# Accumulating DMAs for part of the output sums, idle products up to the first r product, and a new order of operations

## The chip, the cores and the metric

The program runs on one core of a Trainium2 chip. The metric is device microseconds (us) of one execution; the kernel before was timed three times. In the profile TensorE is PE (its weight loads PEld), VectorE is DVE, ScalarE is ACT, GpSimd is POOL and SyncE is SP. SP issues nearly all DMAs; POOL issues the accumulating ones.

## The reference, cut to what matters

Three layers follow one another on 4 sequences of 576 tokens with 512 channels, all in float32.

```python
# 1. attention with 8 heads of 64 channels, each token sees itself and the 63 tokens before it
attn = softmax(mask(q @ k.T / 8));  x = attn @ v                       # (4, 576, 512)
# 2. token shift, then a gated feed-forward
x_prev = shift(x);  xk = mu_k*x + (1-mu_k)*x_prev;  xr = mu_r*x + (1-mu_r)*x_prev
k = relu(xk @ w_k)                                                     # (4, 576, 1024)
x2 = sigmoid(xr @ w_r) * ((k*k) @ w_v)                                 # (4, 576, 512)
# 3. gate from a causal convolution of 5 taps, then two products
gate = sigmoid(sum_j conv_w[j] * x2 shifted by 4-j)
out = (gate * (x2 @ w_val)) @ w_out
```

## The kernel before, in words

Everything is kept transposed: channels on the 128 partitions, tokens along the row. The 2304 tokens are cut into five blocks, t = 0 of 256 tokens and t = 1 to 4 of 512. A unit of attention is one block and one pair of heads, 20 units u0 to u19 (u0 to u3 belong to block 0). A unit goes through these steps, each with a name in the plan: `qk` (scores, PE), `top` (row maximum, DVE), `exp` (ACT), `eps` and `rec` (reciprocal of the row sums), `norm` (DVE), `tp` (transposes on PE into the PSUM tile `at`), `pt` (copy out of PSUM), `pv` (product with v), `x` (copy of the result into `xT`). In block 0 the second half of `at` takes the result of `pv`. From `xT` the steps `a` and `xm` mix each token with the one before. `r`, `h` and `v` are the three products of layer 2. In block 0 they are plain float32 products; in the other blocks each operand is split in two parts (hi, lo) and three products are added.

Weights come in raw and are put together by `w_r ld` (load), `g` (ACT), `t` and `s` (DVE); `w_r s` of the first piece and `xm` of the first two channel groups are what the first `r` product needs.

Layer 3 works on one sequence b = 0 to 3 at a time, as `val{b}` (x2 times w_val) and `out{b}` (times w_out). In `val0` to `val3` and `out0` to `out2` the product is done as seven products of quarter size, m1 to m7, of 12 matmuls each, in `seven` (line 859). They add up in two PSUM banks "u" and "v". What must be used twice is copied from bank u to SBUF: three copies per sequence, `outu` 0, 1 and 2 into the tile `ou` (`valu` for val). For out, three of the four output quarters (00, 11, 01) are then bank v plus one of those copies, added on DVE (`o`, line 951); the quarter 10 is bank u alone, copied by ACT (line 953). `os` stores a quarter of 288 KB. The next sequence's `outu` i waits until the `o` that read the old copy is done. `out3` is a plain product of 96 matmuls and ends the kernel.

The gate of sequences 0 to 2 is worked out early; that of sequence 3 is made late, partly by four accumulating DMAs (`acc`, line 848, 576 KB each) that POOL issues.

No scheduler runs: the table `SLOT` holds a place in the program for each step, the steps are emitted in that order, and each engine executes its own in that order. `Plan.run` walks over the steps with estimated durations, but only for one purpose: where PE would wait longer than `WAIT` ns, `fill` emits idle products (128x128, operands zero, result never read) that keep PE busy, one for every `PASS` ns of the gap less 250 ns. Before, the idle products write to the tile `scores` and end when the first unit of block 1 takes that tile.

Of the kernel before, what the change touches and what calls it, by code (L numbers as in the profile page):

```python
# [36 lines left out]
BY_DMA = (3, 4)  # L37
BIG = 3.0e38
# [4 lines left out]
    'first': '32',  # L43
# [6 lines left out]
    'ldc': '15',  # L50
    'mu': '17',
    'omu': '56',
    'pg': '51',
    'wc0': '69 75 96',
    'wc': '98',
    'first_x': '1',
    'ldqk': '7 3 9 12 13 21 44 81 111 166 195 232 265 295 335 368 393 421 445 495',
    'ldv': '18 10 24 27 46 117 164 185 269 271 298 331 365 389 422 441 499 492 522 577',
    'qk': '20 16 31 34 38 72 106 134 182 227 257 291 330 363 388 417 440 477 491 521',
    'top': '26 22 33 39 48 82 112 149 228 293 296 333 349 376 403 448 450 489 504 535',  # L60
    'exp': '29 25 36 42 59 89 122 168 249 297 311 340 362 384 416 452 457 505 511 545',
    'eps': 'v35 p30 p43 p50 p70 p102 p132 p179 p259 v305 v318 p345 v373 v396 v426 p458 p466 p512 v523 p553',
    'rec': '37 40 55 57 80 103 171 190 262 307 319 355 379 407 432 460 473 517 538 555',
    'norm': '41 45 58 66 92 123 180 196 270 309 320 357 382 410 435 462 485 518 548 583',
    'tp': '47 60 68 85 101 130 189 231 275 314 334 366 392 419 444 480 496 525 558 586',
    'pt': 'a49 v62 a73 a86 a108 a116 a144 a152 a203 a199 a235 a247 a281 a279 a322 a321 a350 a338 v381 a378 a404 '
        'v408 a425 a428 v465 a464 v484 a483 v509 v510 a537 a529 a563 v562 a602 a600',
    'pts': '53 64 78 90 120 155 207 252 287 325 353 383 411 429 469 486 513 541 565 604',
    'pv': '54 65 79 91 125 178 222 255 289 326 358 386 414 437 475 488 519 543 568 632',
    'x': 'v61 a71 v87 v97 a160 a206 a246 a264 a292 v346 a372 a400 v418 v455 v478 a493 a536 v551 a629 v719',  # L70
    'mask': '211 238 278 323 339 370 397 424 447 487 501 531',
    'edge': '218 261 283 329 348 374 401 427',
    'a': 'a83 a100 a110 a118 a230 a237 a272 a276 a352 a356 a436 v439 v494 a498 v610 a614 a693 v764 v768 a797',
    'xm': '88 107 119 126 254 242 300 284 390 367 451 443 520 524 624 620 734 785 776 823',
    'xlo': '93 113 124 129 266 274 327 290 434 415 479 463 609 606 673 634 765 788 783 832',
    'carry': '137 214 260 361 398 459 528 628',
    'r': '94 121 95 115 109 127 139 147 369 395 405 423 590 581 593 599 686 744 751 760 863 871 883 889',
    'sig': '136 138 150 154 399 406 433 438 594 596 603 626 697 752 761 767 873 879 890 909',
    'h': '153 162 165 173 143 148 158 170 176 198 194 205 201 213 210 217 294 301 308 316 337 342 351 377 500 '
        '507 482 532 552 547 561 569 643 672 699 720 695 708 726 737 816 829 802 835 845 859 852 878',  # L80
    'relu': 'v169 a181 a159 a184 a202 a212 a219 a223 a303 a310 v315 v344 v343 a371 v387 a402 v508 v515 v506 a544 '
        'a559 a566 a580 v584 v663 v683 a709 a727 v713 a729 v743 v746 a827 a838 v810 a847 a854 a864 v866 v885',
    'sbuf': '186 188 216 225',
    'slo': 'a193 v191 a221 a229 341 364 385 420 550 567 597 601 707 739 749 759 851 862 877 891',
    'v': '239 251 234 244 263 286 273 277 430 449 446 461 514 527 454 467 635 654 611 625 660 679 607 616 766 '
        '786 780 789 809 824 772 796 919 930 896 905 924 933 901 912',
    'x2': '282 253 299 304 470 471 546 476 661 652 688 627 794 801 830 803 934 914 938 921',
    'st': '336 268 394 391 472 474 549 574 664 655 689 656 805 804 839 843 936 916 947 943',
    'xhi': 'a258 a267 v312 v288 v431 a412 v468 v453 a608 a588 v631 a623 a755 a787 v779 a826',
    'cut': '241 280 360 442 503 619',  # L90
    'shi': '328 347 375 409 534 560 575 585 687 732 738 748 840 848 870 886',
    'sq': 'a332 a359 a380 v413 a540 a564 a595 v592 v696 a736 a740 a754 v846 a857 v874 v888',
    'staging': '0',
    'w_r ld': '19 23',
    'w_r g': '52 74',
    'w_r t': '63 76',
    'w_r s': '67 99',
    'w_r hi': 'v131 a156',
    'w_r lo': '141 161',
    'w_k ld': '84 28 77 114',  # L100
    'w_k g': '140 104 146 177',
    'w_k t': '133 105 128 174',
    'w_k s': '145 135 157 183',
    'w_k hi': 'a197 v167 a240 a215',
    'w_k lo': '208 175 245 220',
    'w_v ld': '151 142 163 192',
    'w_v g': '209 187 243 224',
    'w_v t': '204 172 236 226',
    'w_v s': '233 200 248 256',
    'w_v hi': 'a317 v302 a324 a285',  # L110
    'w_v lo': '354 313 456 306',
    'wide_x': '250',
    'turn': '880',
    'turn_s': '940',
    'turn_w': '834 894',
    'w_val ld': '497 589 578 651',
    'w_val room': '571 636 618 674',
    'w_val g': '572 637 640 675',
    'w_val t': '554 579 582 612 605 622 642 644 648 646 591 667 669 682 670 665 680 710 711 712',
    'w_val s': '576 641 645 678',  # L120
    'w_val hi': 'a613 a650 a684 a714',
    'w_val lo': '615 671 698 721',
    'w_val st': '621 617 668 677 685 702 733 735',
    'w_out ld': '647 681 706 731',
    'w_out room': '701 723 757 775',
    'w_out g': '703 724 793 791',
    'w_out t': '700 716 717 715 718 705 741 742 763 762 773 821 822 831 825 756 815 818 817 849',
    'w_out s': '704 728 820 812',
    'w_out hi': 'v747 a769 v833 v853',
    'w_out lo': '753 771 837 869',  # L130
    'w_out st': '750 758 777 774 836 842 875 872',
    'wv2': '898 899',
    'wo2': '900 897 917 945',
    'ldx': '884 941 957 1011',
    'gbuf': '881 942 1020 1082',
    'ldg': '882 958 1060',
    'xhi_': 'a931 a906 a907 a904 v918 a928 a959 a991 a966 a964 a997 a988 a993 a1076 a1032 a1038 a1088 a1073 a1100 '
        'a1162 a1119 a1118 a1171 a1161',
    'xlo_': '935 908 910 915 954 939 963 1008 968 974 1005 998 1023 1084 1052 1061 1095 1081 1106 1181 1144 1137 '
        '1178 1163',  # L140
    'xsum': '902 903 911 926 960 961 975 984 1017 1030 1065 1071 1111 1115 1154 1158',
    'val': '937 944 948 951 955 965 969 973 983 989 999 1006 1021 1028 1041 1053 1063 1080 1087 1096 1102 1110 '
        '1121 1141 1148 1166 1187 1182',
    'valu': 'a946 v952 a962 a978 a1002 a1013 a1048 a1079 a1092 a1127 a1157 a1176',
    'valc': '949 967 970 979 994 1019 1027 1035 1072 1097 1104 1113 1132 1180 1208 1191',
    'gv': '950 971 972 992 1003 1025 1031 1045 1090 1109 1107 1129 1183 1201 1209 1194',
    'ghi_': 'v953 a1009 a980 a982 a985 a1007 a1004 a1039 a1066 a1029 a1036 a1042 a1056 a1068 a1122 a1136 a1124 '
        'a1147 a1145 a1174 v1175',
    'glo_': '956 1018 1015 986 990 1010 1014 1049 1069 1067 1040 1057 1075 1078 1135 1150 1185 1159 1156 1188 '
        '1177',  # L150
    'gsum': '976 981 996 1000 1033 1037 1054 1062 1120 1142 1165 1170',
    'out': '977 1046 995 1012 1016 1024 1034 1059 1074 1070 1091 1108 1116 1128 1138 1155 1160 1173 1179 1192 '
        '1197 1202 1211 1207 1213 1216 1220 1219 1221',
    'outu': 'a987 a1001 a1022 a1064 a1077 a1112 a1149 a1169 a1184',
    'o': '1055 1026 1044 1043 1086 1123 1130 1146 1168 1186 1198 1203 1214 1217 1222 1224',
    'os': '1058 1051 1047 1050 1134 1153 1133 1151 1172 1190 1200 1205 1215 1218 1223 1225',
    'tap': '1083 1089 1099 1085 1093 1101 1098 1125 1140 1103 1117 1139',
    'part': '1094 1114 1131 1152',
    'acc': '1105 1126 1143 1167',
    'gate': '1164 1189',  # L160
    'ghi': 'a1193 a1196 a1210 v1204',
    'glo': '1195 1199 1212 1206',
    'cld': '481 587 676 781 813 868',
    'ctap': '502 526 530 533 557 490 516 539 542 556 598 630 633 639 658 638 649 653 657 659 690 692 722 730 770 '
        '691 694 725 745 778 795 798 806 807 811 790 792 799 800 808 828 841 844 850 856 855 858 860 861 865 '
        '887 893 895 913 925 892 920 922 923 927',
    'cgate': '570 662 782 814 867 929',
# [1046 lines left out]
```

## Time and profile before

| | |
|---|---|
| three runs | 422.95, 423.63, 421.28 us; median 422.95 |
| the profiled execution | 423.3 us, of which its span (first to last instruction) is 421.5 us |
| instructions | 9145 |
| PE busy | 410.9 us (97% of the span) |
| DVE busy | 351.9 us (83%) |
| ACT busy | 256.7 us (61%) |
| POOL busy | 22.5 us (5%) |
| mean granted TensorE clock | 0.996 |
| DMA | 77.69 MB, mean 184 GB/s |

Busy is the time in which an engine executes something; a busy PE can still be slow, when its granted clock is 0.5 (1.2 GHz in place of 2.4 GHz) or when its matmuls are small. The chain that ended last gives PE 83% and DVE 13% of the span.

### The profile page before, as it was taken

Reading aid. Unit: us, or ns where it says so; the run is one execution under the profiler, and the core shown is the slowest. Engines: PE = TensorE matmul, PEld = TensorE weight load, DVE = VectorE, ACT = ScalarE, POOL = GpSimd, SP = SyncE. Lnnn points to the kernel's source line nnn. Section 1 sums busy time; section 2 is a strip of 40 time slices with the busy share of each in tenths; the row PEclk is TensorE's granted clock in tenths of the full one; section 3 lists DMA queues with packets and bytes.
Section 4 is the critical chain, followed back from the end, with each engine's and each line's share of the span. In section 5 each row is a group of like instructions: output and inputs, shape, how many; then the busy total and the mean of one; then the engine's idle time right before and its main releaser. Section 6 shows DMA issues by size and latency. Waiting matters only on the chain.

```text
span 421.5 us, 9145 instructions
## 1 busy us (share of the span) xinstructions
PE 410.9 (97%) x3746; PEld 354.8 (84%) x3746; DVE 351.9 (83%) x511; ACT 256.7 (61%) x585; POOL 22.5 (5%) x62
## 2 busy tenths in 40 slices
PE   8789999999999999999999999999999999999996
PEld 6578888888888888888888888888888899999996
DVE  3899998988989799458978996988584999999970
ACT  4899997789996175765334645154223284577721
POOL 2114101000002000000000000000000000001000
PEclk9899999999999999999999999999999999999999
DMA  8998925333432522072375434434997913616622
GB/s 306 407 366 320 381 64 166 104 117 104 131 113 98 208 103 77 2 286 89 116 261 210 137 157 155 161 152 153 343 427 286 400 69 114 225 35 155 176 86 112
DMA packets 24714, 77.69 MB, mean 184 GB/s; under 512 B 2528, under 2 KB 3296, under 8 KB 22624
## 3 DMA queue, kind: packets, MB, share of 16 engines
q1 hardware_dynamic: 23952, 74.74, 48.5%
q0 software_dynamic: 576, 2.36, 2.9%
q8 instruction: 29, 0.48, 0.4%
q14 instruction: 13, 0.11, 0.1%
q10 hardware_dynamic: 144, 0.00, 0.0%
HBM read 53.90 MB, written 20.84 MB: 177 GB/s over the span
## 4 chain that ended last, share of the span: by engine, by line
PE 83%; DVE 13%; issue 1%; ACT 1%; ACTq 0%; POOL 0%; DVEq 0%; POOLq 0%
PE h L603 21%; PE v L603 21%; PE r L603 10%; PE at L497 4%; PE ao L512 4%; PE scores L433 4%; PE v L627 3%; PE h L627 3%; PE out L979 3%; PE out2m L873 3%; DVE x L771 2%; DVE gq L771 2%; PE val3m L873 2%; PE r L627 2%; DVE early L914 1%; DVE xt L761 1%
## 5 line engine op out<-in xcount | busy, mean ns | idle before, releaser
L603 PE MATMUL h<-x,wk 128*128 128x512 f32 x384 | 90.7, 391 | 0.0
L603 PEld LDWEIGHTS h<-x,wk 128*128 128x128 f32 x384 | 71.5, 188 | 14.8
L603 PE MATMUL v<-sh,wv 128*128 128x512 f32 x256 | 81.1, 390 | 0.0
L603 PEld LDWEIGHTS v<-sh,wv 128*128 128x128 f32 x256 | 48.1, 188 | 10.0
L603 PE MATMUL v<-sl,wv 128*128 128x512 f32 x128 | 49.8, 389 | 0.0
L603 PE MATMUL r<-x,wr 128*128 128x512 f32 x192 | 45.4, 391 | 0.0
L603 PEld LDWEIGHTS r<-x,wr 128*128 128x128 f32 x192 | 35.7, 188 | 7.3
L804 DVE SCALAR_TENSOR_TENSOR early<-early,wc 128x576 f32<-128x576 f32 x48 | 38.2, 810 | 3.1 <-ACT early L802 2.7
L476 ACT ACTIVATE s<-s,m 128x128 f32<-128x128 f32 x96 | 37.2, 397 | 4.6 <-DVE m L465 4.6
L603 PEld LDWEIGHTS v<-sl,wv 128*128 128x128 f32 x128 | 24.0, 188 | 4.9
L504 ACT ACTIVATE pt<-at 128x512 f32<-128x512 f32 x28 | 16.4, 601 | 13.6 <-PE at L497 13.6
L654 ACT ACTIVATE rk<-h 128x512 f32<-128x512 f32 (+1 forms) x23 | 12.1, 538 | 17.9 <-PE h L603 15.8
L563 DVE SCALAR_TENSOR_TENSOR xm<-xT,omu,xm 128x512 f32<-128x512 f32 x32 | 22.5, 744 | 0.6 <-POOL xT L569 0.6
L684 DVE TENSOR_TENSOR sl<-rk,sh 128x1024 fp32r<-128x1024 f32 x16 | 19.4, 1219 | 3.9 <-ACT rk L682 3.8
L706 DVE TENSOR_TENSOR sgs<-v,sgs 128x512 f32<-128x512 f32 (+1 forms) x20 | 12.5, 632 | 10.9 <-PE v L603 10.9
L678 ACT ACTIVATE sh<-rk 128x1024 fp32r<-128x1024 f32 x16 | 16.9, 1055 | 6.8 <-DVE rk L656 6.7
L512 PEld LDWEIGHTS ao<-pt,vt 128*64 128x64 f32 x512 | 16.2, 138 | 5.5 <-issue 2.8
L586 DVE TENSOR_TENSOR x<-xm,x 128x1024 fp32r<-128x1024 f32 x16 | 19.4, 1219 | 1.2 <-ACT x L583 1.1
L486 DVE TENSOR_TENSOR s<-s,m 128x1024 f32<-128x1024 f32 x16 | 19.5, 1219 | 0.2
L768 ACT ACTIVATE x<-xt 128x576 fp32r<-128x576 f32 x15 | 10.0, 677 | 15.4 <-DVE xt L761 9.4
L476 ACT ACTIVATION_READ_ACCUMULATOR s<-s,m 128x1 f32 x96 | 18.8, 196 | 0.0
L512 PE MATMUL ao<-pt,vt 128*64 128x64 f32 x512 | 18.4, 225 | 0.0
(200 smaller groups left out, 857.5 us busy)
## 6 DMA issues: line engine op xcount, KB each, us to landing
qk<-qk SPq DMA_DIRECT2D x16, 544.0 KB, 5.2
vt<-vh SPq DMA_DIRECT2D x16, 512.0 KB, 4.9
xb<-x2d SPq DMA_DIRECT2D x4, 1152.0 KB, 7.2
out_t<-st SPq DMA_DIRECT2D x15, 288.0 KB, 2.8
x2d<-sgs SPq DMA_DIRECT2D x16, 256.0 KB, 3.5
w_out<-w SPq DMA_DIRECT2D x8, 512.0 KB, 3.5
w_val<-w SPq DMA_DIRECT2D x8, 448.0 KB, 4.5
wk<-w_val SPq DMA_DIRECT2D x2, 1792.0 KB, 11.8
```

Of the source, the lines that this page charges most:

```text
L433: PE.matmul(a["ps"][rows, h, o:o + W + HW], lhsT=a["q"][heads[h], c * HW:(c + 1) * HW], rhs=a["k"][heads[h], c * HW:c * HW + W + HW], star ...
L476: ACT.activation(out=s, in_=scores()[:, c // n2, c % n2, :] if by_pe else s, func=AF.Exp, scale=D ** -0.5 if by_pe else 1.0, bias=l(0)[:, ...
L486: lambda: V.tensor_tensor(out=a["s"], in0=a["s"], in1=l(1).unsqueeze(2).to_broadcast(sq), op=ALU.mult))
L512: PE.matmul(a["o"][heads[h], c * W:(c + 1) * W], lhsT=a["v"][:, c, heads[h]], rhs=a["pt"][:, h, c * W:(c + 1) * W], start=True, stop=True)
L563: V.scalar_tensor_tensor(out=m, in0=xT[:, f, :n], scalar=omu[:, c:c + 1], in1=m, op0=ALU.mult, op1=ALU.add)
L586: lambda E: E.tensor_tensor(out=dst(1), in0=src(), in1=f32(dst(0)), op=ALU.subtract))
L603: PE.matmul(ps, lhsT=a, rhs=b[:, kt, :], start=(kt == 0 and i == 0), stop=(kt == nk - 1 and i == 2))
L627: PE.matmul(Ps[key][:, :n], lhsT=ws(kt), rhs=x()[:, kt, :], start=kt == 0, stop=kt == nk - 1)
L678: ACT.activation(out=Ss[t][0][:, f, :n], in_=rk(), func=AF.Square)
L684: lambda E: E.tensor_tensor(out=Ss[t][1][:, f, :n], in0=rk(), in1=f32(Ss[t][0][:, f, :n]), op=ALU.subtract))
L804: V.scalar_tensor_tensor(out=o, in0=x, scalar=c, in1=o, op0=ALU.mult, op1=ALU.add)
L873: PE.matmul(z[bank][:, j, :HS], lhsT=lhs, rhs=rhs, start=new and kt == 0 and e == 0, stop=kt == 1 and e == 2, skip_group_check=not new)
```

## The change: what it does

It does four things.

1. For sequences 1 and 2 (`ADDED`) the quarters 00, 11 and 01 are no longer added on DVE. ACT copies bank v to SBUF, SP stores it as before, and a new step `oa` on POOL then issues a DMA that adds the SBUF copy `ou` onto the stored result in DRAM. `oa` waits for the landing of that store, and the next sequence's `outu` waits for `oa`.
2. Idle products go to an unused part of the second half of `at`, and are emitted until the first `r` product or the first `pt` of block 1 is reached.
3. `WAIT` goes from 700 to 400 and `PASS` from 430 to 250: shorter gaps are filled, and a gap of the same length gets more products. `WARM` stays at 900.
4. Nearly every place in `SLOT` is new, and some steps that DVE or ACT can both do have moved from one to the other.

```diff
+ADDED = (1, 2)
...
-    WAIT, PASS, WARM = 700, 430, 900
+    WAIT, PASS, WARM = 400, 250, 900
...
-            if "at" not in Q:
-                Q["at"] = pa.tile([P, 2, TB], F32, tag="at", name="at")
...
-        prev = lambda h, p: [({"val": "gv", "out": "o"}[mul], b - 1, h, p)] if b else []
+        prev = lambda h, p: [({"val": "gv", "out": "oa" if b - 1 in ADDED else "o"}[mul], b - 1, h, p)] if b else []
...
-                if u:
+                if u and b not in ADDED:
                     V.tensor_tensor(out=o, in0=ps(), in1=u(), op=ALU.add)
                 else:
                     ACT.activation(out=o, in_=ps(), func=AF.Copy)
...
             store(b, h, p, [slice(0, 2)])
+            if u and b in ADDED:
+                op(("oa", b, h, p), "pool", 1000, [("os", b, h, p), *deps], lambda: G.dma_start(
+                    out=out[2 * b + h, :, 2 * p:2 * p + 2, :], in_=u(), accum_op=ALU.add), moves=1750)
...
     def first_idle():
-        idle["ps"] = Q["scores"] = pq.tile([P, 2, TB], F32, tag="qk", name="scores")
+        Q["scores"] = pq.tile([P, 2, TB], F32, tag="qk", name="scores")
+        Q["at"] = pa.tile([P, 2, TB], F32, tag="at", name="at")
...
-        if any(k in Ps for k in [("r", 0, m) for m in range(NF)]) or HP in A and "ps" in A[HP] or n <= 0:
+        if any(k in Ps for k in [("r", 0, m) for m in range(NF)]) or any("pt" in A[u] for u in A if u >= HP) or n <= 0:
             return
         for _ in range(n):
-            PE.matmul(idle["ps"][:, 0, :P], lhsT=warm, rhs=warm, start=True, stop=True)
+            PE.matmul(Q["at"][:, 1, TA:TA + P], lhsT=warm, rhs=warm, start=True, stop=True)
```

Of `SLOT`, the orders that the prediction speaks of, written out as sequences of steps on an engine up to the first `r` product (u0 to u3 are the units of block 0):

```
PE  before: qk u1, qk u0, qk u2, qk u3, qk u4, tp u0, pv u0, tp u1, pv u1, tp u2, qk u5, pv u2, tp u3, pv u3, r
PE  after:  qk u1, qk u0, qk u2, qk u4, qk u3, tp u0, pv u0, tp u1, pv u1, tp u2, qk u5, pv u2, tp u3, pv u3, r
DVE before: top u1, top u0, top u2, eps/rec u0, top u3, rec u1, norm u0, norm u1, top u4, rec u2, omu, rec u3, norm u2,
            x u0, pt u1, w_r0 t, norm u3, w_r0 s, w_r1 t, rec u4, top u5, x u2, xm 0.0r
DVE after:  omu, top u1, top u0, eps/rec u1, norm u1, top u2, rec u0, norm u0, top u3, top u4, rec u2, x u0, norm u2,
            pt u1, rec u3, w_r0 t, norm u3, x u1, eps u4, pt u2, rec u4, w_r0 s, top u5, xm 0.0r
```

And in layer 3 the quarters, `oa` and the last products:

```
POOL after: acc 0, oa1 00, acc 1, acc 2, oa1 01, oa1 11, acc 3, oa2 00, oa2 01, oa2 11
last products before: out3 00, 01, 10, 11      after: out3 01, 00, 11, 10
val0 on DVE before: x differences S1 and S2 of val1, lo of val1's first pair, quarter 11      after: S1, S2, quarter 11
```

## Rows read from the trace of the kernel before

**Rows 1.** Five stretches of the span: length, each engine's busy us (instructions), clock, DMA
```profile
0.00:23.10 23.10, 17.67 (x395) 13.35 (x395) 14.35 (x36) 16.29 (x66) 3.78 (x16) 0.93 0.94 359
23.10:331.60 308.50, 308.50 (x2729) 257.96 (x2728) 261.40 (x366) 190.10 (x440) 14.96 (x41) 1.00 0.51 184
331.60:404.60 73.00, 71.76 (x532) 70.74 (x531) 72.62 (x106) 46.94 (x74) 3.72 (x5) 1.00 0.48 147
404.60:417.60 13.00, 12.95 (x98) 12.71 (x96) 3.56 (x6) 2.66 (x5) 0.00 (x0) 1.00 0.25 94
417.60:421.50 3.90, 0.00 (x0) 0.00 (x0) 0.00 (x0) 0.69 (x2) 0.00 (x0) 1.00 0.40 147
```

**Rows 2.** Timeline, PE at the start: start, duration, engine, operation, count, [idle before]
```profile
0.99 2.93 PE L1158 MATMUL scores<-sgs 128*128 128x128 f32 x12 [0.99 <-POOL sgs L302]
...
4.26 0.89 PE L433 MATMUL qk<-early 64*32 64x96 f32 x32
...
8.07 0.56 PE L433 MATMUL qk<-early 64*32 64x96 f32 x32
...
11.82 0.53 PE L433 MATMUL scores<-qk 64*32 64x96 f32 x21 [0.71 <-issue]
...
16.07 1.05 PE L512 MATMUL at<-pt,sgs 128*64 128x64 f32 x16 [1.18 <-DVE pt L505]
...
17.05 1.12 PE L497 MATMUL at<-ident,xm 128*128 128x128 f32 x4
...
19.99 0.69 PE L512 MATMUL at<-pt,rk 128*64 128x64 f32 x16
...
20.60 0.66 PE L497 MATMUL at<-ident,xm 128*128 128x128 f32 x4
...
23.08 1.99 PE L627 MATMUL r<-x,words 128*128 128x256 f32 x8
```

**Rows 3.** Timeline, DVE at the start: one row for each kind of step
```profile
5.26 0.69 DVE L467 TENSOR_REDUCE first_m<-qk 128x4 f32<-128x512 f32 x1 [2.11 <-PE qk L433]
...
12.39 1.22 DVE L467 TENSOR_REDUCE m<-scores 128x8 f32<-128x1024 f32 x1
...
13.73 0.17 DVE L484 RECIPROCAL first_m<-first_m 128x4 f32<-128x4 f32 x1
...
13.95 0.67 DVE L486 TENSOR_TENSOR xm<-xm,first_m 128x512 f32<-128x512 f32 x1
...
14.99 0.42 DVE L518 COPY xT<-at 128x256 f32<-128x256 f32 x1 [0.37 <-PE at L497]
...
17.13 1.22 DVE L345 SCALAR_TENSOR_TENSOR words<-words,x 128x1024 int32<-128x1024 int32 x1
...
22.32 0.87 DVE L563 SCALAR_TENSOR_TENSOR x<-xT,omu,x 128x256 f32<-128x256 f32 x2
```

**Rows 4.** Chain of waits, ACT's exponentials of the first two units: start, us, line, count
```profile
6.25 2.91 ACT xm L476 x15
```

**Rows 5.** Timeline, PE late: the two longest waits
```profile
332.67 1.85 PE L873 MATMUL val0m<-x,wk 128*128 128x288 f32 x12 [0.74 <-ACT early L885]
...
385.00 0.40 PE L873 MATMUL out2m<-gq,wr 128*128 128x288 f32 x1 [0.34 <-DVE gq L771]
```

**Rows 6.** Line L848, the accumulating DMAs of the gate: POOL's issue in ns, and landing
```profile
L848 POOL DMA_DIRECT2D gate<-tt x2: 859/938/1016, 376.1 to 387.6; - x2
...
DMA to landing us min/median/max: 4.8/4.8/4.9
```

**Rows 7.** Line L931 from 414 us, then from 418.2 us: the last stores' issue to landing
```profile
DMA to landing us min/median/max: 2.1/2.1/2.1
...
DMA to landing us min/median/max: 1.7/1.8/1.8
```

**Rows 8.** Timeline, ACT at the end: copies of the last quarters out of PSUM
```profile
416.03 0.65 ACT L989 ACTIVATE st<-out 128x576 f32<-128x576 f32 x1 [4.20 <-PE out L979]
...
417.58 0.71 ACT L989 ACTIVATE st<-out 128x288 f32<-128x288 f32 x2 [0.90 <-PE out L979]
```

More of the change, by code (lines that the diff above doesn't have):

```diff
@@ L953, in go @@
                     ACT.activation(out=o, in_=ps(), func=AF.Copy)
-            op(("o", b, h, p), "dve" if u else "act", v_ns(QN) if u else p_ns(QN), [*deps, *room(b, h, p)], go)
+            by_v = u and b not in ADDED
+            op(("o", b, h, p), "dve" if by_v else "act", v_ns(QN) if by_v else p_ns(QN), [*deps, *room(b, h, p)], go)
             store(b, h, p, [slice(0, 2)])
+            if u and b in ADDED:
+                op(("oa", b, h, p), "pool", 1000, [("os", b, h, p), *deps], lambda: G.dma_start(
+                    out=out[2 * b + h, :, 2 * p:2 * p + 2, :], in_=u(), accum_op=ALU.add), moves=1750)
         seven("out", b, "g", gq, lambda c, j: w2["w_out"](c, j)[:, 1:], WO, "turn_s", use)
@@ L1144, in tile_kernel @@
         early_gate(n, SPLIT[n // 2], n % 2)
-    idle = {}
     def first_idle():
-        idle["ps"] = Q["scores"] = pq.tile([P, 2, TB], F32, tag="qk", name="scores")
+        Q["scores"] = pq.tile([P, 2, TB], F32, tag="qk", name="scores")
+        Q["at"] = pa.tile([P, 2, TB], F32, tag="at", name="at")
     op("idle", "none", 0, ["warm"], first_idle)
     def fill(t, n):
-        if any(k in Ps for k in [("r", 0, m) for m in range(NF)]) or HP in A and "ps" in A[HP] or n <= 0:
+        if any(k in Ps for k in [("r", 0, m) for m in range(NF)]) or any("pt" in A[u] for u in A if u >= HP) or n <= 0:
             return
         for _ in range(n):
-            PE.matmul(idle["ps"][:, 0, :P], lhsT=warm, rhs=warm, start=True, stop=True)
+            PE.matmul(Q["at"][:, 1, TA:TA + P], lhsT=warm, rhs=warm, start=True, stop=True)
     plan.fill = fill
```

237 rows, old and new, of the table SLOT are left out of this document.

## The prediction, made before the changed kernel was run

> **What bounds the kernel now.** I read the stretches of the span first. In them the reader is to see four parts: a start of 23.1 us in which PE is busy for 17.67, with a mean clock of 0.93; 308.5 us in which PE has not one idle 0.01 us and the full clock; 73 us in which PE has 71.76 and DVE 72.62, so that both are full; and an end of 13.0 us of products plus 3.9 us after the last of them [rows 1]. The work of PE is the same before and after (idle products aside), so whatever this change does to the time, it does by PE's waits: 5.4 us in the start, 1.24 us in the 73, and the 3.9 behind the last product. In the middle nothing can be gained, only lost.
>
> Then I read the timeline of the start. The first r product begins at 23.08 us, and from there PE never waits [rows 1, 2]. So the start is worth what the first r product moves. Ahead of it PE runs idle products from 0.99 (12 records in 2.93 us: a float32 product shows as two, so six products), then the scores of the units; the scores of one unit take 0.89 us at first and 0.56 later [rows 2]: the first ones run at 1.2 GHz, the later ones at 2.4. Later the clock falls once more: a pv of 16 products takes 1.05 us at 16.07 and 0.69 at 19.99, a tp 1.12 at 17.05 and 0.66 at 20.60 [rows 2]. A mean clock of 0.93 over 23.1 us is about 3.2 us at half speed [rows 1]. Ahead of the fall PE had waited much: 1.18 us just before, and 0.71 us in the middle of the scores of u4, with nothing that released it [rows 2].
>
> **The change part by part.**
>
> *More idle products in the first gap.* The number is the gap less 250 ns, divided by PASS. Six at 430 means that 2.58 to 3.01 us were to be filled; at 250 that makes 10 to 12, I take 11. Five more, 0.49 us each (2.93 / 6) at 1.2 GHz, are 2.4 us; as the last of them and the scores behind them come close to the rise of the clock, the next scores take 0.56 in place of 0.89. I take 1.5 us by which the first unit's row maximum starts later: 6.8 us in place of 5.26 [rows 2, 3]. Bounds: 0.5 (the clock has risen early) and 2.4. This is the one place where the change puts work on the path that sets the start. What waits behind is the first maximum on DVE, and ACT's exponentials behind that.
>
> *New order up to the first r product.* PE's list differs in one place only (scores of u4 ahead of those of u3); DVE's and ACT's lists are new. I walk them with the old durations. Maximum of u1: 6.8 + 0.69 + 0.17 = 7.7. Exponentials: two units took 2.91 [rows 4], so 1.45 each, and that of u1 ends at 9.1. That frees the buffer for the scores of u2 (0.56 and its masks, 0.9): 10.1. From there DVE is the queue that counts: maximum of u2, rec and norm of u0, 0.86 + 0.17 + 0.67, until 11.9; then it waits for the scores of u3, which PE reaches behind those of u4 (about 1.4) at 12.4. Then without a pause: top u3 0.86, top u4 1.39, two rec 0.34, two x 0.84, two norm 1.34, two pt (same width as norm) 1.34, w_r0 t 0.67 (an estimate, as norm), eps and rec of u4 0.34, w_r0 s 1.22, top u5 1.39, xm 0.87 [rows 3]. That is 10.6 us, and r starts at 23.0. Before, the same queue began 1.5 us earlier and lost it in waits: it did norm u0 only behind top u3, and waited for PE at half clock. So the later start and the better order cancel: **0.0 us**. Low bound: what PE lost at half clock on pv and tp alone is 0.36 + 0.46, with the scores between them about 1.2, and the wait of 0.71 [rows 2]; if both go and the first gap costs nothing, -1.9. High bound: the 1.5 is not made good and the wait of 0.71 comes again, now ahead of u3's maximum too: +2.2.
>
> *Idle products in the later gaps.* They fill what PE waits anyway, with 250 ns left free each time, so they cost nothing as long as the gaps come as planned; if a gap is shorter, the cover is gone, and one product too many costs 0.2 us at 2.4 GHz. They hold the clock, which is in the walk above already.
>
> *The order from 23 to 331 us.* Before, no wait in 308.5 us, with DVE at 85% and ACT at 62% [rows 1]. A step moved between them changes nothing as long as it comes in time; whether each does is not to be seen in this trace. I take **0.0**, with bounds of 0 and +1.2 (as much as PE waits in the 73 us where DVE is as full as PE).
>
> *The six sums taken off DVE.* Six additions of some 0.75 us, 4.5 us in all, leave DVE, and six copies of 0.65 [rows 8] go to ACT, which is busy for 46.94 of the 73 us [rows 1] and has room. But PE is busy for 71.76 of the same 73, so at most 1.24 us can come of it. PE's longest wait there (0.74 at 332.67) is for a copy of its own m7 result ahead of m4, in sequence 0, where nothing is moved. That of 0.34 at 385.00 is for DVE [rows 5] and goes. In val0 the quarter 11 now comes ahead of a longer DVE step, which takes a smaller wait. **-0.4 us**, bounds -1.24 and 0.
>
> *The accumulating DMAs.* Six issues on POOL at 0.94 us, on an engine that is busy for 3.72 of 73 us [rows 1, 6]. Each waits for a store (landing 2.1 to 4.8) and must land before the next sequence's copy into the same part of `ou`. The trace has no accumulation onto DRAM; the nearest rows are a store of the same 288 KB (2.1, [rows 7]) and an accumulation of 576 KB into SBUF (4.8, [rows 6]); I take 4.8, the nearer kind. Copy, store, issue and accumulation: 0.65 + 4.8 + 0.94 + 4.8 = 11.2 us. For quarter 00 there are ten products of some 1.6 us in between (1.85 with the tail of the last matmul, [rows 5]), 16 us: hidden. For quarters 01 and 11 of sequence 1, POOL holds them behind two `acc`, and between their issue and the copy that needs the room lie four to five products, about 7 us against 0.94 + 4.8 = 5.7: hidden by little. Those of sequence 2 have 13 us of out3 and 3.9 us behind them and free no buffer. **0.0**, bounds 0 and +3.
>
> *The end.* The last store is now quarter 10 whole; before it was quarter 11 in two halves. Before: 417.58 + 0.71, then a landing of 1.75. After: 0.65, then 2.1 [rows 7, 8]. **+0.2 us**.
>
> Sum: 0.0 + 0.0 - 0.4 + 0.0 + 0.2 = -0.2 us on the 423.3 of the profiled execution, of which 421.5 are the span. That execution is 0.35 above the median of the runs shown; on the median it makes 422.95 - 0.2 = **422.7 us**.
>
> The row says that POOL's issues took 0.86 to 1.02 us and landed in 4.8 to 4.9, beside a DVE that is busy for 72.62 of 73 us [rows 1, 6]. The Trainium skill ("SBUF — State Buffer", section "A bandwidth-pool intuition that's wrong (but worth ruling out)") speaks against such DMAs: GpSimd can't write their descriptors while certain VectorE copies hold the shared port, and one of 620 ns took 3100. By that rule each could land some 2.5 us later (an estimate from that page), and the margin for quarters 01 and 11 would be gone; by the row it is not so here. It is why the third rival has any chance beyond a few per cent.
>
> **The rivals.**
>
> *Faster start.* The idle products keep PE at 2.4 GHz from 6 us on, the first unit starts hardly later, and the 0.71 goes. For it: pv and tp at half clock lie in line ahead of the first r product. Against it: five more products at 1.2 GHz stand ahead of the first scores. -1.9 - 1.24 + 0.2 = -2.9: 420.0 us.
>
> *Slower start.* One mechanism: the products added to the first gap. They hold PE until about 6 us although the first scores could start at 3.9, and every step of DVE behind moves with them, as its queue has no pause left to take it up. It decides against the change from the point where the delay of the first maximum is above 1.5 us and the wait in u4's scores comes too. +2.2 + 0.2 = +2.4: 425.3 us.
>
> *Accumulations late.* The copies `outu` 1 and 2 of sequence 2 find `ou` not yet free, and PE stops between m6 and m4 of out2. For it: the margin of 1 to 2 us. Against it: landings in rows 6 hardly vary. +3.0 - 0.2: 425.7 us.
>
> *Doesn't do what it says.* The idle products share a PSUM bank with the results of pv; if they wait for the reads of it, the clock still falls. Then the start costs about 1.2 more: 423.9 us, still no change by the measure below.
>
> **How the numbers follow.** Forecast 0.46 and the last rival 0.06, both within 0.5% (2.1 us, about what a measurement of this kernel can tell from no change: 420.8 to 425.1); faster start 0.29; slower start 0.12; accumulations late 0.07. So faster 0.29, same 0.52, slower 0.19. The forecast's own range is -1.5 to +1.5, 421.2 to 424.2. For 8 in 10 it must take in most of the faster case and the edge of the slower ones: 419.8 to 425.0.
>
> **What would show it.** First scores at about 5.7 us in place of 3.9, first row maximum at 6.8; over 40 records of idle products in place of 22, and no stretch at half clock between 6 and 23 us; the first r product at 22 to 24 us; PE without a wait from there to 331 us; PE's waits from 331 to 405 us near 0.8 in place of 1.24; six new DMAs on POOL that land in 4.8 us or less, and no copy into `ou` that waits for one; some 0.2 us more behind the last product. The forecast is wrong if r starts before 21.5 or after 24.5, or if PE waits for over 1 us anywhere between 24 and 405 us.

## The result, and the profile after

After the change the kernel takes 427.75 us (median of 4 runs, 426.06 to 429.29), beside 422.99 (4 runs) for the kernel before on the same chip: 1.0127 of it, 95% interval 1.0085 to 1.0168. Forecast were 422.7 us and a range of 419.8 to 425.0: the change costs 4.8 us, where no difference was the likeliest case.

The profiled execution took 429.22 us, its span 427.4. Its stretches, cut at the same work as those of before [rows 1]; the columns are the stretch, its length, busy us (instructions) of PE, PEld, DVE, ACT and POOL, the granted clock, the DMA share and GB/s:

```profile
0.00:28.90 28.90, 23.41 (x428) 18.80 (x428) 15.57 (x38) 16.08 (x67) 2.63 (x15) 0.82 0.88 326
28.90:338.75 309.85, 309.85 (x2731) 257.97 (x2728) 259.69 (x367) 191.48 (x441) 7.79 (x40) 1.00 0.51 178
338.75:410.40 71.65, 70.86 (x532) 70.62 (x531) 69.20 (x100) 51.20 (x80) 7.22 (x9) 1.00 0.62 175
410.40:423.40 13.00, 12.94 (x98) 12.70 (x96) 2.48 (x5) 2.67 (x5) 1.76 (x2) 1.00 0.58 146
423.40:427.40 4.00, 0.00 (x0) 0.00 (x0) 0.00 (x0) 0.65 (x1) 0.00 (x0) 0.99 0.31 117
```

Against [rows 1] the start is 5.8 us longer, at a clock of 0.82 in place of 0.93; the 308.5 us are 1.35 longer although PE is busy in every one of them; the 73 us are 1.35 shorter; the end hardly moves. So one stretch holds the loss, and two small ones cancel.

The timeline of PE in the start (start, duration, operation, count, [idle before]):

```profile
0.99 4.18 PE L1161 MATMUL at<-sgs 128*128 128x128 f32 x22 [0.99 <-POOL sgs L304]
5.11 0.31 PE L425 MATMUL qk<-low,one 64*64 64x256 bf16 x4
...
6.61 2.05 PE L1161 MATMUL at<-sgs 128*128 128x128 f32 x16
...
12.34 0.19 PE L429 MATMUL qk<-low,one 64*64 64x64 bf16 x1 [1.42 <-issue]
...
14.43 1.22 PE L1161 MATMUL at<-sgs 128*128 128x128 f32 x4 [0.69 <-ACT pt L504]
15.58 1.12 PE L512 MATMUL at<-pt,sgs 128*64 128x64 f32 x16
...
19.20 2.08 PE L1161 MATMUL at<-sgs 128*128 128x128 f32 x8 [0.78 <-DVE pt L505]
21.21 1.12 PE L512 MATMUL at<-pt,sgs 128*64 128x64 f32 x16
...
27.43 0.94 PE L1161 MATMUL at<-sgs 128*128 128x128 f32 x6 [1.01 <-ACT xT L519]
28.30 0.69 PE L512 MATMUL at<-pt,rk 128*64 128x64 f32 x16
28.91 0.92 PE L627 MATMUL r<-x,words 128*128 128x256 f32 x3
```

Line L1161 holds the idle products. The reader is to look at the last three groups of them: each has a wait in front of it, for a copy out of the tile `at`, and only then runs, ahead of the `pv` for which the gap was. The gap stays and the products come on top: 15.58 - 14.43 = 1.15, then 2.01, then 0.87, together 4.0 us. The clock is at 1.2 GHz all the same from the first of them on (`pv` takes 1.12; [rows 2] have 1.05 at that clock and 0.69 at 2.4).

DVE, which the prediction took for the queue that counts from the maximum of u3 on, stands still behind PE there (the first row is that maximum, the others are its three longest pauses up to the first r product):

```profile
13.27 0.69 DVE L469 TENSOR_REDUCE first_m<-qk 128x4 f32<-128x512 f32 x1 [1.99 <-PE qk L435]
...
16.82 0.42 DVE L518 COPY xT<-at 128x256 f32<-128x256 f32 x1 [1.25 <-PE at L512]
...
18.46 0.69 DVE L505 COPY pt<-at 128x512 f32<-128x512 f32 x1 [0.61 <-PE at L497]
...
23.42 0.42 DVE L518 COPY xT<-at 128x256 f32<-128x256 f32 x1 [3.01 <-PE at L497]
```

Late, PE keeps one wait of the two longest of [rows 5], the one of sequence 0; that for DVE is gone. The second fence holds the new DMAs (their issue in ns min/median/max, first and last start, and their landing), the third the landing of the last three stores, the fourth ACT at the end.

```profile
339.87 3.46 PE L873 MATMUL val0m<-x,wk 128*128 128x288 f32 x24 [0.79 <-ACT early L885]
```

```profile
L958 POOL DMA_DIRECT2D out_t<-ou x6: 858/875/1204, 382.2 to 415.7; - x6
DMA to landing us min/median/max: 4.4/6.0/7.2
```

```profile
DMA to landing us min/median/max: 1.8/1.8/2.1
```

```profile
423.42 0.65 ACT L993 ACTIVATE st<-out 128x576 f32<-128x576 f32 x1 [0.93 <-ACT st L993]
```

The accumulations land in 4.4 to 7.2 us, up to 2.4 more than the 4.8 of [rows 6]; no copy into `ou` waits for one.

For all kernels below, the same four stages, taken from the timeline: the start of the first r product, from there to the first value product (`val0`), from there to the start of the last matmul, and what lies behind it (us; the kernel's profiled execution, one each).

| kernel | first r | to val0 | to last matmul | behind | span | clock |
|---|---|---|---|---|---|---|
| before | 23.08 | 300.70 | 93.47 | 4.3 | 421.5 | 0.996 |
| after | 28.91 | 302.02 | 92.11 | 4.4 | 427.4 | 0.988 |
| no_late_idle | 24.47 | 302.11 | 92.11 | 4.4 | 423.1 | 0.992 |
| two_tiles | 24.78 | 301.87 | 92.11 | 4.4 | 423.2 | 1.000 |
| old_idle | 26.13 | 302.14 | 92.11 | 4.4 | 424.8 | 0.986 |
| idle_alone | 25.34 | 301.26 | 93.47 | 4.3 | 424.3 | 0.998 |
| first_gap | 23.04 | 300.68 | 93.47 | 4.3 | 421.5 | 1.000 |
| late_gaps | 24.16 | 300.69 | 93.47 | 4.3 | 422.6 | 0.999 |
| no_added | 25.65 | 301.81 | 94.62 | 4.4 | 426.5 | 0.999 |
| added_alone | 22.15 | 300.68 | 97.24 | 4.3 | 424.3 | 0.996 |
| old_until_val | 21.34 | 300.72 | 93.63 | 4.4 | 420.1 | 1.000 |
| old_until_val_no_added | 21.16 | 300.70 | 95.39 | 4.6 | 421.9 | 0.999 |
| old_until_r | 21.61 | 303.83 | 92.11 | 4.4 | 422.0 | 0.998 |
| old_until_760 | 23.31 | 302.26 | 92.11 | 4.4 | 422.1 | 0.996 |
| old_until_640 | 21.06 | 300.75 | 92.11 | 4.4 | 418.3 | 0.999 |
| tp_apart | 23.04 | 309.36 | 93.48 | 4.3 | 430.1 | 0.995 |

One thing has to be known to read the first column: from one run of a kernel to the next the granted clock differs, and with it the start, and each row is one run. Of 23 runs of before on one chip, 19 have a clock of 0.998 to 1.000 and spans of 419.8 to 420.6, four 0.995 or 0.996 and 421.5 to 421.8; the profiled one is of the second kind. Of the four of after, two have 0.998 (424.3, 424.5) and two 0.988 (427.4 each). So at the full clock the change costs 424.4 - 420.2 = 4.2 us, and 3.0 more in the runs that lose the clock.

### The profile page after: what moved, and what is told of

Its sections match the earlier page's. It is cut to its first block, busy times and chain, and to the rows that moved or that the text cites. A ratio compares the mean times of both kernels' runs of the same rounds, so it can differ in the third digit from the quotient of the medians.

```text
span 427.4 us, 9208 instructions
## 1 busy us (share of the span) xinstructions
PE 417.1 (98%) x3780; PEld 360.1 (84%) x3780; DVE 346.9 (81%) x508; ACT 262.1 (61%) x592; POOL 19.4 (5%) x66
## 4 chain that ended last, share of the span: by engine, by line
PE 97%; issue 1%; ACT 1%; DVE 0%; POOL 0%; ACTq 0%; DVEq 0%; POOLq 0%
PE h L603 21%; PE v L603 21%; PE r L603 10%; PE at L497 4%; PE ao L512 4%; PE scores L435 4%; PE h L627 3%; PE v L627 3%; PE out L983 3%; PE val0m L873 3%; PE out2m L873 3%; PE val3m L873 3%; PE out1m L873 3%; PE val2m L873 3%; PE out0m L873 3%; PE val1m L873 3%
## 5 line engine op out<-in xcount | busy, mean ns | idle before, releaser
L654 ACT ACTIVATE rk<-h 128x512 f32<-128x512 f32 (+1 forms) x32 | 17.1, 549 | 33.5 <-PE h L603 30.7
L449 DVE SCALAR_TENSOR_TENSOR s<-scores,cap 128x1024 f32<-128x1024 f32 x12 | 14.6, 1220 | 9.6 <-PE at L497 9.5
L583 ACT ACTIVATE x<-xm 128x1024 fp32r<-128x1024 f32 x14 | 14.8, 1057 | 7.8 <-DVE xm L563 7.8
```

What stands on the lines that cost most here:

```text
L654: ACT.activation(out=o, in_=ps, func=AF.Relu)
```

## The experiments

Theory 1: the start is lost to idle products that wait for copies out of the tile they write to, and then stand ahead of work. Theory 2: it is lost by the new order. Then, for the later stages: which part gives the late gain and which takes the 1.3 us of the middle.

**No idle products in the later gaps** (no_late_idle):

```diff
-any("pt" in A[u] for u in A if u >= HP)
+any("pt" in A[u] for u in A)
```

> The changed kernel, but idle products end at the first pt (that of u0), so the three bursts ahead of pv u0, pv u1 and pv u3 are gone; those of the first gaps stay. Theory 1 (idle products wait for copies out of the same PSUM tile, stand ahead of pv and push it back): the three bursts held pv for 1.15, 2.0 and 0.87 us, so the first r product comes some 4 us earlier, at 25 us or before, and the time falls to about 423.5. Theory 2 (the new order up to the first r product is what costs): r stays later than 27.5 us and the time at 426 or more.

**Their own tile** (two_tiles): the halves of `at` become two tiles.

```diff
-Q["at"] = pa.tile([P, 2, TB], F32, tag="at", name="at")
+Q["at"] = [pa.tile([P, TB], F32, tag=f"at{i}", name=f"at{i}") for i in range(2)]
```

> The changed kernel with its idle products, but the PSUM tile at is two tiles of one bank each. Theory 1: the wait comes from the two halves being one tile; now idle products start as soon as PE reaches them, pv waits for its own pt alone, no stretch at half clock is left after the first rise, r comes at 24.5 us or before, time about 422.5. Theory 2: r later than 27.5 us, time 426 or more. If the waits stay although the tiles are apart, theory 1 has the wrong mechanism.

**The order alone** (old_idle): after with the idle products as before.

```diff
-WAIT, PASS, WARM = 400, 250, 900
+WAIT, PASS, WARM = 700, 430, 900
...
-any("pt" in A[u] for u in A if u >= HP)
+HP in A and "ps" in A[HP]
...
-PE.matmul(Q["at"][:, 1, TA:TA + P], lhsT=warm, rhs=warm, start=True, stop=True)
+PE.matmul(Q["scores"][:, 0, :P], lhsT=warm, rhs=warm, start=True, stop=True)
```

> The changed kernel with the idle products of the kernel before (target scores, WAIT 700, PASS 430, end at the first scores of block 1), so the new order and the accumulating DMAs alone. Theory 1: r at 23 to 24.5 us, time 422 to 424. Theory 2: r later than 27.5 us, time 426 or more.

**The idle products alone** (idle_alone): the same lines the other way round, in before.

> The kernel before with nothing but the new idle products (target at, WAIT 400, PASS 250, end at the first pt of block 1). Theory 1: r moves from 23.1 to 26 us or later, time 426 to 428. Theory 2: r within 1 us of 23.1, time 422 to 424.

Measured against before: 425.66 us, 1.0077 [1.0052, 1.0102] for no_late_idle; 425.07, 1.0062 [1.0039, 1.0085] for two_tiles; 425.34, 1.0064 [1.0038, 1.0090] for old_idle; 426.04, 1.0087 [1.0060, 1.0114] for idle_alone. The first two times lie between the 423.5 and 422.5 of Theory 1 and the 426 of Theory 2, so the first r products decide. no_late_idle has lost the clock in all four runs (0.989 to 0.992), like the profiled after, and its first r product is 4.4 us earlier. two_tiles has the full clock; no_added below, whose start is that of after, has it too in its profile, and against that the first r product is 0.9 earlier. PE in two_tiles:

```profile
14.61 0.61 PE L1161 MATMUL at<-sgs 128*128 128x128 f32 x4
15.46 0.69 PE L512 MATMUL at<-pt,sgs 128*64 128x64 f32 x16 [0.24 <-ACT pt L504]
...
23.30 0.94 PE L1161 MATMUL at<-sgs 128*128 128x128 f32 x6 [1.08 <-ACT xT L519]
24.78 1.99 PE L627 MATMUL r<-x,words 128*128 128x256 f32 x8
```

The first group now runs inside the gap and leaves 0.24 of it, as it was meant to; the last one still waits, since the copy `xT` reads the half that the idle products write. So products that wait for their own tile are a part of the loss (Theory 1), and a tile of their own mends one of the three places in full. But neither run comes back to before. old_idle gives another part: two of its ten runs have the full clock and spans of 420.5 and 421.4, the other eight 0.986 to 0.990 and 422.5 to 425.6. The order of the start by itself costs little at the full clock, and loses the clock more often than before's (8 of 10 runs, against 5 of 14 of before on the same chip). One row of its PE timeline, and one of its windows (columns as in the stretches above):

```profile
12.93 0.52 PE L435 MATMUL qk<-early 64*32 64x96 f32 x19 [2.42 <-issue]
```

```profile
15.00:17.50 2.50, 1.73 (x19) 1.54 (x20) 1.78 (x5) 2.50 (x16) 0.19 (x1) 0.50 1.04 408
```

Behind a stall of 2.42 us, which nothing in the profile released, the clock is 0.50. So Theory 2 holds in part, through the clock. idle_alone keeps the clock in three of four runs (0.998 or more; the fourth has 0.996) and costs 3.9 us in those, 424.2 against the 420.3 of before's nine at that clock on the same chip: here holding the clock is not worth its price.

**Which of the idle products** (first_gap, late_gaps): before, with the closer spacing in the first gap alone; and before, with the spacing of the first gap as it was, the closer one behind it, and the target `at` and the end of after.

```diff
 def fill(t, n):
     ...
+    plan.WAIT, plan.PASS = 700, 430   # first_gap; in late_gaps 400, 250
     for _ in range(n):
```

> Before, with the closer spacing of the idle products (one for each 250 ns) in the first gap alone; later gaps, the tile they write and the order as before. Theory 1 (the first gap is a cost by itself: the added products stand ahead of the first scores and nothing behind them takes the delay up): first scores at 5.9 us in place of 3.9 and the first r product about 2 us later than in a run of before at the full clock (23.4 to 23.9 in place of 21.4 to 21.9), ratio 1.005. Theory 2 (the first gap is taken up by waits behind it, and only the products in the later gaps cost): r at 21.4 to 22, ratio 1.000.

> Before, with idle products in the unused part of the tile at up to the first r product; the first gap is filled as before (one for each 430 ns), only the later ones closer (250 ns, from 400 ns of gap). Theory 1 (both parts cost, about 2 us each, as the two together made 4 in idle_alone at the full clock): r at 23.2 to 23.7, ratio 1.005. Theory 2 (only the later ones cost): r at 25, ratio 1.009. If the later ones hold the clock and cost nothing: r at 21.4, ratio 0.998.

Measured: first_gap 423.32 us, 1.0037 [1.0023, 1.0050]; late_gaps 424.40, 1.0061 [1.0048, 1.0073]. All runs of both have the full clock: median spans of 421.5 and 422.6 beside 420.0 of before's nine runs, so +1.5 and +2.6. PE in first_gap, and in late_gaps:

```profile
0.99 4.83 PE L1159 MATMUL scores<-sgs 128*128 128x128 f32 x22 [0.99 <-POOL sgs L302]
...
6.01 0.56 PE L433 MATMUL qk<-early 64*32 64x96 f32 x32
```

```profile
13.92 0.71 PE L1158 MATMUL at<-sgs 128*128 128x128 f32 x4 [0.69 <-ACT pt L502]
14.56 0.69 PE L510 MATMUL at<-pt,sgs 128*64 128x64 f32 x16
...
17.02 0.94 PE L1158 MATMUL at<-sgs 128*128 128x128 f32 x6 [1.18 <-DVE pt L503]
...
22.90 0.71 PE L1158 MATMUL at<-sgs 128*128 128x128 f32 x4 [1.24 <-DVE xT L516]
```

In first_gap the first scores come at 6.01 in place of 4.26 [rows 2]; nothing behind takes the 1.75 up but 0.25 of it. In late_gaps the waits are those of before (0.69, 1.18, 1.20 to 1.24), whole, and the products behind them add 0.64, 0.86 and some 0.6: 2.1 of the 2.6.

**The sums back on DVE** (no_added): after, with

```diff
-ADDED = (1, 2)
+ADDED = ()
```

**The DMAs alone** (added_alone): before with the lines of `ADDED` as in after, and in `SLOT`

```diff
-'os': '1058 1051 1047 1050 1134 1153 1133 1151 1172 1190 1200 1205 1215 1218 1223 1225',
+'os': '1058 1051 1047 1050 1088 1153 1133 1151 1172 1190 1200 1205 1215 1218 1223 1225',
+'oa': '1088 1153 1151 1172 1190 1205',
```

**Before's order up to val0** (old_until_val, and the same without `ADDED`), and **up to the first r product** (old_until_r): before's table for the steps below a slot, after's for the rest, with the idle products of before.

```diff
+head = [step for step in places(OLD) if slot < CUT]     # CUT 937, 937, 94
+return head + [step for step in places(SLOT) if step not in head]
```

> After with the sums of sequences 1 and 2 back on VectorE (ADDED empty, the six DMA places taken out of the order), all else as after. Theory 1a (the DMAs give the late gain): late stage 93.3, span 428.5, ratio 1.016. Theory 1b (the order gives it): late stage 92.1, as after: ratio 1.013.

> Before, with the six sums in accumulating DMAs and nothing else changed but one store that SP issues earlier; each accumulation is issued as soon as its store has landed. Theory 1 (the DMAs give the gain of the late stage whatever the order, as old_until_val against old_until_val_no_added shows, 1.8 us, and no_added against after, 2.5): late stage 92.1 to 92.6, ratio 0.997. Theory 2 (they give it only in an order searched with them; in an order searched without them the sums stood where VectorE had room): late stage 93.2 to 94, ratio 1.000 or a little above, and a wait of TensorE for a copy of ScalarE or for a copy that waits on an accumulation.

> The idle products and the order of before up to the second pair's value product (slot 936 of before), from there the order of after, with the six sums in accumulating DMAs. Theory 1 (everything lost was lost ahead of the value products; behind them the change gains): first r product at 23.1 us, from there to the value product 300.7, from the value product to the last matmul 92.1 where before took 93.47, tail 4.4: span 420.2, 0.997 of before. Theory 2 (the late order works only behind the early one, since the copies that it finds done were done earlier by it): the late stage 93 to 93.5, ratio 1.000.

> As old_until_val, but the sums of sequences 1 and 2 stay on VectorE, in the places that the copies have in the order of after; no accumulating DMA. Theory 1a (the DMAs give the gain of the late stage: six sums less on a VectorE that is busy 96 per cent of it): late stage about 93.3, ratio 1.000. Theory 1b (the late order gives it, the DMAs nothing): 92.1, ratio 0.997. Tail 4.3 rather than 4.4 by either, if the last store alone sets it.

> The idle products and the order of before up to the first r product (slot 93), then the order of after with the accumulating DMAs. First r at 23.1. Theory 1 (the order of after costs 1.3 us between the first r product and the value product by itself, since TensorE changes its kind of work more often there): middle 302.0, late 92.1, tail 4.4: span 421.6, ratio 1.000. Theory 2 (the 1.3 us are a debt of the late start, weights and copies that come behind it): middle 300.7, span 420.3, ratio 0.997.

Measured: no_added 428.86 us, 1.0162 [1.0135, 1.0190]; added_alone 425.26, 1.0079 [1.0065, 1.0093]; old_until_val 422.43, 1.0012 [0.9992, 1.0033]; without `ADDED` 424.33, 1.0046 [1.0030, 1.0062]; old_until_r 422.88, 1.0019 [1.0001, 1.0038]. The DMAs give 94.62 - 92.11 = 2.5 us in the order of after and 1.8 in the mixed one; in the order of before they take 3.8 (Theory 2 of added_alone). The waits of PE late in no_added (total, times, longest), then added_alone's wait in PE's timeline, ACT's copy that it waited for, and two windows around it:

```profile
PE val0m L872 <- ACT early L884: 0.8, 1, 0.8
PE out L982 <- ACT st L952: 0.7, 1, 0.7
PE val3m L872 <- DVE x L770: 0.4, 1, 0.4
PE out1m L872 <- DVE st L950: 0.4, 1, 0.4
```

```profile
397.78 0.58 PE L875 MATMUL out2m<-gq,wr 128*128 128x288 f32 x2 [1.96 <-ACT ou L887]
```

```profile
397.07 0.65 ACT L887 ACTIVATE ou<-out2m 128x576 f32<-128x576 f32 x1 [3.25 <-DMA out_t<-ou]
```

```profile
395.00:400.00 5.00, 3.04 (x17) 2.81 (x16) 1.59 (x3) 2.34 (x4) 1.35 (x2) 0.81 1.08 231
400.00:404.00 4.00, 4.00 (x27) 4.00 (x26) 3.90 (x7) 2.89 (x4) 0.00 (x0) 0.81 0.93 200
```

The copy into `ou` waits 3.25 us for an accumulation, PE 1.96 for the copy, and over these 9 us the mean clock is 0.81. That is the prediction's rival of late accumulations, in the place it named; in the order of after it doesn't occur.

old_until_val lost the late gain in its profile: PE waits there 0.7 for a step of DVE in `val0` that before's order had left behind. That profile is the longest of its six runs at the full clock (419.2 to 420.1), so the others may have kept a part. old_until_r kept the gain, but with a middle of 303.83, of which 1.4 is a wait of PE for a step of DVE ahead of an `h` product. The other six of its runs at 0.998 or more span 419.9 to 420.6, where the profiled one has 422.0; without that wait its middle is 302.4, near the 302.0 of its Theory 1.

**Ten transposes behind the next product** (tp_apart): in before's table ten `tp` that stood directly behind the scores of a later unit change places with the product behind them; of unit 10, on PE:

```diff
-qk u12, tp u10, h 20
+qk u12, h 20, tp u10
```

> Before, with ten of the transposes that stood directly behind the scores of a later unit moved behind the product that follows them (the two change places), as the order of after has it. Theory 1 (a change of TensorE from small to large products costs about 0.11 us each, so the order of after pays for nine more of them in the middle): the stage from the first r product to the value product 301.7 to 301.9 in place of 300.7, with no wait of TensorE, ratio 1.0025. Theory 2 (the middle of after is longer for another reason): 300.7, ratio 1.000.

Measured 432.0 us, 1.0235 [1.0220, 1.0250]; the middle is 8.7 longer, some 6 of it new waits of PE (2.3 in three waits for `pt` alone). So it decides nothing on the 1.3 us, and shows only that before's order doesn't bear these ten moves.

**The cut elsewhere** (old_until_640, behind the last `pv`, and old_until_760), else as old_until_val:

```diff
-CUT = 937
+CUT = 640     # and 760
```

> The idle products and the order of before up to slot 639 of before (by there every transpose and every scores product is done), from there the order of after, with the accumulating DMAs. Theory 1 (the 1.3 us of the middle belong to the place of the transposes among the products, ahead of the cut; the shorter late stage needs the order of after only behind it): middle 300.7, late 92.1, tail 4.4: span about 418.8 in place of 420.1, ratio 0.997. Theory 2 (the middle's cost lies behind the cut too, or the late stage needs the earlier order as well): middle 301.3 to 302 or late 93.5, ratio 1.000.

> As old_until_640 with the cut at slot 760, in the last block's first products. Theory 1: as there, span about 418.8, ratio 0.997. Theory 2 (the closer the cut lies to the late stage, the less of its gain is left, as the cut at 937 left none): late stage between 92.1 and 93.6.

Measured: old_until_640 420.81 us (12 runs), 0.9972 [0.9955, 0.9989], a little faster than both kernels; old_until_760 421.82, 0.9990 [0.9970, 1.0010]. In old_until_640 the middle is that of before and the late stage that of after; PE's only wait from 24 us to the end is that of sequence 0:

```profile
PE val0m L1009 <- ACT early L1021: 0.8, 1, 0.8
```

old_until_760 has the late stage of after too, but a middle of 302.26: PE waits at 58.5 us for DVE (0.35) and at 252.0 for ACT (0.48), and the starts at these two places come 1.3 us later in all. So the cut must be well chosen, and the late gain does not need all of the order of after behind slot 640. From old_until_640 and old_until_r, the 1.3 us lie in the steps between slots 94 and 640, among the attention units. What they consist of stands in PE's timeline, first old_until_640 over one unit (order of before), then after:

```profile
104.69 1.15 PE L648 MATMUL ao<-pt,vt 128*64 128x64 f32 x32
105.77 1.00 PE L571 MATMUL scores<-qk 64*32 64x96 f32 x64
106.70 1.09 PE L633 MATMUL at<-ident,s 128*128 128x128 f32 x8
107.55 5.70 PE L739 MATMUL r<-x,wr 128*128 128x512 f32 x24
113.17 1.15 PE L648 MATMUL ao<-pt,vt 128*64 128x64 f32 x32
```

```profile
110.28 1.15 PE L512 MATMUL ao<-pt,vt 128*64 128x64 f32 x32
111.36 1.00 PE L435 MATMUL scores<-qk 64*32 64x96 f32 x64
112.28 3.02 PE L603 MATMUL h<-x,wk 128*128 128x512 f32 x12
115.14 1.04 PE L497 MATMUL at<-ident,s 128*128 128x128 f32 x8
115.93 5.73 PE L603 MATMUL r<-x,wr 128*128 128x512 f32 x24
121.59 1.15 PE L512 MATMUL ao<-pt,vt 128*64 128x64 f32 x32
```

From one `pv` to the next 8.48 us, and 11.31. The second holds twelve more products; at 0.227 between the starts of two products inside a group that is 2.72, which leaves 8.59. The same work with one more change between small and large products takes 0.11 us longer, without any idle time. Over the middle PE changes 78 times in place of 69, so nine more are worth about 1.0 of the 1.3. The starts of the whole middle say the same: in the groups of products that begin behind such a change, the second start comes about 0.1 us later than the usual 0.227 (0.216 in block 0), at 29 places of after against 19 of before, 2.88 us against 1.81 in all. This is read from the intervals; no run changed it alone, so the cause is argued and not shown.

## Why the prediction was wrong, point by point

- *Idle products in the later gaps*, "they cost nothing as long as the gaps come as planned": this step failed, +2.6 at the full clock (late_gaps). The gaps came as planned in late_gaps. But the products wait for the copies that end the gap, so they fill none of it. The fourth rival named this wait and then priced only the clock that would be lost (1.2), not the products' own place ahead of `pv`.
- *The first gap and the order up to the first r product*, "the later start and the better order cancel": failed too. The first gap was sized right (+1.5 of delay, measured +1.5), but the order gave nothing back: with before's idle products and the full clock its first r product comes at 420.5 - 302.1 - 92.1 - 4.4 = 21.9 us, or 22.8 in the other run, where before's on the same chip comes at 420.3 - 300.7 - 93.5 - 4.3 = 21.8 (all three worked out from spans). The walk over DVE's queue began from a start of before that had lost the clock, and counted as a gain of the order what a run of before at the full clock has anyway. Its 10.6 us from the maximum of u3 to r hold where DVE need not wait for PE: 14.29 to 24.78 in two_tiles, 10.5. In after they are 13.27 to 28.91, 15.6, as DVE pauses for PE by 1.25, 0.61 and 3.01: "without a pause" is what failed. The stall that the high bound named (0.71, now ahead of u3's maximum) came too, with 1.42. The slower start was a rival, at +2.4; its mechanism, the first gap, is 1.5 of the 4.1 measured.
- *They hold the clock*: in two of four runs they did not, 3.0 us each. Those runs pull the median up. That they hold it more often than not has support: in the order of after the clock was lost in 12 of 14 runs without the later ones (no_late_idle, old_idle) and in 3 of 14 with them (after, two_tiles, no_added), though not all on one chip. They cost more than that saves: after at the full clock spans 424.3 and 424.5, no_late_idle without it 423.1 to 424.9.
- *The order from 23 to 331 us*, 0.0 with a bound of 1.2: mis-sized, +1.3. PE does not wait there, as forecast; what was left out is that its own work can get longer without a wait, by what the intervals show with the number of changes between kinds.
- *The six sums*, -0.4 within -1.24: mis-sized, -1.36 with the order. The bound counted PE's idle time. The distances between the starts of successive matmuls are 2.45 us above their usual 0.133, summed over ten distances of before's late stage (five waits, two distances each), and 1.05 after, in two: some waits are too short to show as idle time, and behind each wait the next start comes about 0.1 later. What the DMAs are worth in it hangs on the order: 2.5 gained in that of after, 3.8 lost in that of before.
- *The accumulating DMAs*, 0.0: right, though by less than was worked out, as landings went to 7.2 and not 4.8. The rival had +3.0; where it came true (added_alone) it was 3.8. The rule weighed there, that VectorE can keep GpSimd from writing descriptors (the Trainium skill, "SBUF — State Buffer", section "A bandwidth-pool intuition that's wrong (but worth ruling out)"), has no support here: POOL issued in 0.86 to 1.20 us beside a DVE busy for 69.20 of 71.65; the longest landing, 7.2 us, is that of the last of the six, issued at 415.66 us, when DVE had nothing left to do since 412.9. It was issued 0.6 behind another, which landed in 4.4; what made the landings longer no run tells.
- *The end*, +0.2: right, 4.40 behind the last matmul's start in place of 4.27.

At the full clock the terms add up to 420.0 + 1.5 + 2.6 + 1.3 - 1.4 + 0.1 = 424.1, and after has 424.3 and 424.5. That it comes so close is in part luck: both costs of the idle products were measured in the order of before, and the 0.1 to 1.0 that the order of the start costs by itself is left out.

## What to carry to other kernels

An idle product can be free only if nothing it touches is read by the copy that ends the gap, and even then not where it outlasts the gap, as in the first one: ask of each what it waits for and what stands behind it in the queue, before asking what it does for the clock. Price each stage of a new order on its own and against a run at the same clock; here two of its stages lost and one gained, and the one spliced in alone was faster than either kernel. An engine without idle time can still get slower; here, as far as the intervals tell, by changing more often between kinds of work.

## What was not expected of the hardware

- The same program loses TensorE's clock in some runs and not in others: of before 5 of 14, 0 of 9, 4 of 23 and 3 of 23 runs on four chips, of old_idle 8 of 10 on the first of these chips, of late_gaps none of five on the second, where before loses none either. Two runs of before on the fourth chip were long (421.1 and 421.9) at a clock of 1.000, so the clock isn't all that differs. Ahead of the fall in before, after, no_late_idle and old_idle PE had stalled for 0.71, 1.42, 1.06 and 2.42 us, between 10 and 13 us, with nothing in the profile to release it; two_tiles (1.39) and no_added (1.01) had such a stall and kept the clock. In the order of before the stall was 0.17 to 0.98 in the profiled runs, in that of after 1.01 to 2.42. Its cause stays open.
- Around a wait of 1.96 us late in the kernel the clock was 0.81 over 9 us, and the stage 3.8 us longer, not 2.
- Six accumulations of 288 KB onto DRAM landed in 4.4 to 7.2 us, where plain stores of that size took 2.1 [rows 7].
